# Six spectral sums handed from VectorE to accumulating DMAs, a seven-product down projection for a sixth unit, and a new order table

## The chip, the cores and the metric

The kernel runs on one core of one Trainium2 chip. The metric is the device time of one execution in microseconds, and lower is better. Before the change it is 338.21 us (median of 3 runs, 338.10 to 338.67).

## The reference

Two layers stand one behind the other, and both use the same weights. A layer is a gated long convolution (block A) and a gated feed-forward (block B), each with a layer norm in front and a residual sum behind. Tokens S = 2048, channels D = 512, feed-forward width F = 1792, everything bf16:

```python
def _A_ref(q, k, v, shift_k, ssm_k, ssm_D):
    ...                       # k_shift: causal convolution of k with 4 taps per channel
    kv = k_shift * v
    L = 2 * S
    ...                       # kv_f, kf_f: real FFTs over 2S of kv and of ssm_k, padded with zeros
    y_f = kv_f * kf_f[None, :, :, :]
    y = irfft2(y_f, ...)[:, 0, :S, :]     # causal convolution over all 2048 tokens
    y = y + kv * ssm_D[None, None, :]
    return q * y

def _B_ref(x, w_gate, w_up, w_down):
    g = _silu(x @ w_gate)
    u = x @ w_up
    return (g * u) @ w_down

x = A_q
x = x + _A_ref(_layernorm(x), A_k, A_v, A_shift_k, A_ssm_k, A_ssm_D)
x = x + _B_ref(_layernorm(x), B_w_gate, B_w_up, B_w_down)
x = x + _A_ref(_layernorm(x), A_k, A_v, A_shift_k, A_ssm_k, A_ssm_D)
x = x + _B_ref(_layernorm(x), B_w_gate, B_w_up, B_w_down)
```

The long convolution's result y depends on k, v and the filter alone, so it is computed once and used by both layers.

## The kernel before, in words

**Convolution.** The 2048 tokens are cut into NB = 4 blocks of 512. Block i of k*v gets a spectrum X[i], and two neighbouring blocks of the filter get one spectrum G[j]. Each is a tile of 128 partitions by 4096 bf16 values (1 MB): 4 slots of a real and an imaginary part of 512 channels each. The spectrum of output block k is Z[k], the sum of X[i]·G[j] over i + j = k. `product(i, j)` makes one of these terms on VectorE (DVE): two multiplications of 128x4096 (line L765, into tiles t1 and t2), and two combinations of 128x2048 (L769), a subtraction and an addition. The first product of a block writes its combinations into Z[k]. Each later one writes them back into t1, and one more DVE instruction of 128x4096 (L773) adds t1 to Z[k]. There are six of these: one for Z[1], two for Z[2], three for Z[3]. `inverse(k)` then folds Z[k] (L653, then L659 and L670, on DVE), multiplies by the inverse tables on TensorE (PE), and ScalarE (ACT) copies y out of PSUM.

**Feed-forward.** A unit (layer, c, h) is one of the two halves, 256 tokens, of block c in a layer; there are 16. `prologue` normalises, multiplies by y, adds to x, takes the statistics of the second norm, normalises to z, and has SyncE's queue (SP) transpose z into zT by DMA (L1006). `ffn` runs over four groups of 4, 4, 4 and 2 tiles of 128 of the 1792 columns: gate and up products on PE, silu and a copy on ACT (L1197, L1198, L1258, L1262), their product on DVE (L1204, L1267), and the down projection on PE. Some groups are computed with the tokens in rows, and their product hr is turned into sg by two DMA transposes from SP (L1206). The plain down projection is 28 matmuls of 512 columns for a unit (L1287), and ACT copies (L1332) and one DVE addition (L1339) bring it into x.

**Seven products.** For the units in the table STRASSEN, `seven` takes for two column tiles and two token rows seven products of 256 columns where the plain form takes eight (as 4 matmuls of 512). The operands need sums in front: on DVE three instructions a group (L1076, L1078, L1080, into cb), and once for all units sums of the down weights (L1061). The results land in four PSUM banks, and `add_seven` brings them into x with four ACT copies (L1109) and five DVE instructions (L1114 to L1121). Before the change five units work in this way: (1,2,1), (0,3,0), (0,3,1) and (1,3,0) in all four groups, (1,3,1) in two.

**Statistics.** A norm's mean and variance come either from DVE (L926, L927) or from ACT (L941, L950, L954); the tables ST1 and ST2 choose per unit. GpSimd (POOL) raises the variance to the power -1/2 (L912) for both.

**Order.** No scheduler decides at build time what runs when: every step is recorded with its engine, a cost and its buffers, and the table ORDER gives each step its place. Engines follow that order, each on its own queue, and wait for each other by semaphores. `walk` replays the steps with their costs in that order and chooses the buffer slot of each tile; in it a DMA transpose that is issued beside a load lands later (`late == 2` and `landed`).

Of the kernel before, what the change touches and what calls it, by code (L numbers as in the profile page):

```python
# [9 lines left out]
P = 128  # L10
# [11 lines left out]
ST2 = lambda l, c, h: (l, c, h) in {(0, 0, 0), (0, 2, 1), (1, 2, 1)}  # L22
K_ACT = lambda b: b in {2, 3}
PW = 0.7
# [6 lines left out]
STRASSEN={(1,2,1):4,(0,3,0):4,(0,3,1):4,(1,3,0):4,(1,3,1):2}  # L31
# [1574 lines left out]
```

## Time and profile before

| what | value |
|---|---|
| runs | 338.67, 338.10, 338.21 us; median 338.21 |
| profiled execution | span 337.1 us from the first to the last instruction; its own time is not on the page, and the median run is 1.1 us above its span |
| TensorE (PE) | busy 332.4 us (99% of the span), 2300 matmuls recorded |
| VectorE (DVE) | busy 314.3 us (93%), 566 instructions |
| ScalarE (ACT) | busy 269.4 us (80%), 550 instructions |
| GpSimd (POOL) | busy 36.1 us (11%), 48 instructions |
| DMA | 31.08 MB, mean 92 GB/s |
| granted PE clock | 1.00 |

Matmuls follow each other before the one ahead has ended: 4 matmuls of 512 columns start within 0.86 us, though each of them counts as 379 ns. So a matmul's price is read from the chain (time for a number of matmuls in a row), and a DVE instruction's price from the starts in the timeline, not from the mean length.

### The profile page before, as it was taken

The page shows a single profiled execution, that of the slowest core. Times are in us where ns is not written, and L with a number is a line of the kernel's source. Part 1 is how long each engine was busy: PE and PEld are TensorE (multiplying, and loading weights), DVE is VectorE, ACT ScalarE, POOL GpSimd, SP SyncE. Part 2 cuts the span into 40 slices and gives each one's busy share as a digit, 9 for nine tenths or more (in the row PEclk, how much of TensorE's full clock was granted, in tenths as well). Part 3 has the DMA queues.
Part 4 walks back from the last instruction along what each step waited for, and adds up shares of the span by engine and source line. Part 5 has one row for each costly group of instructions (what it writes and reads, how often), then busy time and mean ns, then how long its engine had stood idle before and what let it go on. Part 6 is the DMA issues. An engine that isn't in the chain of part 4 may idle for free.

```text
span 337.1 us, 6249 instructions
## 1 busy us (share of the span) xinstructions
PE 332.4 (99%) x2300; PEld 208.0 (62%) x2300; DVE 314.3 (93%) x566; ACT 269.4 (80%) x550; POOL 36.1 (11%) x48
## 2 busy tenths in 40 slices
PE   9999999999999999999999999999999999999996
PEld 7665865645445564644545474654445787878994
DVE  7799999999999999999999999997898998986995
ACT  6999999999966684989999794989765748476862
POOL 4010100031210100022110200021000000000000
PEclk9999999999999999999999999999999999999999
DMA  7999403632354446253314433320415320203001
GB/s 278 331 281 387 65 3 77 140 93 34 78 94 86 95 88 146 72 80 74 69 33 83 104 81 102 81 53 10 84 33 95 65 65 16 42 8 64 2 33 62
DMA packets 75817, 31.08 MB, mean 92 GB/s; under 512 B 67589, under 2 KB 73610, under 8 KB 75786
## 3 DMA queue, kind: packets, MB, share of 16 engines
q1 hardware_dynamic: 75632, 30.61, 38.3%
q8 instruction: 18, 0.29, 0.4%
q14 instruction: 13, 0.11, 0.1%
q10 hardware_dynamic: 154, 0.07, 0.1%
HBM read 12.33 MB, written 2.10 MB: 43 GB/s over the span
## 4 chain that ended last, share of the span: by engine, by line
PE 85%; DVE 10%; ACT 2%; issue 1%; POOL 0%; POOLq 0%
PE pf L423 48%; PE pd L1287 19%; PE ps L1097 7%; PE ps L423 6%; PE pf L1171 4%; DVE t L755 1%; PE wm L1572 1%; DVE Z L759 1%; DVE bst L926 1%; DVE t L769 1%; ACT jk L950 1%; DVE Z L773 1%; DVE t L765 1%; DVE m L896 1%; DVE z L976 1%
## 5 line engine op out<-in xcount | busy, mean ns | idle before, releaser
L423 PEld LDWEIGHTS <-zT 128*128 128x128 bf16 x496 | 48.5, 98 | 55.1 <-issue 0.2
L423 PE MATMUL pf<-wu_sb,zT 128*128 128x512 bf16 x248 | 61.5, 379 | 0.0
L423 PE MATMUL pf<-wg_sb,zT 128*128 128x512 bf16 x248 | 61.4, 379 | 0.0
L423 PE MATMUL pf<-zT,wg_sb 128*128 128x256 bf16 x400 | 50.7, 273 | 0.3 <-DVE zT L1037 0.3
L1197 ACT ACTIVATE sg<-pf 128x512 bf16<-128x512 f32 x62 | 37.4, 615 | 14.9 <-PE pf L423 10.7
L1287 PE MATMUL pd<-wd_sb,sg 128*128 128x512 bf16 x200 | 48.9, 379 | 0.0
L1198 ACT CAST hr<-pf 128x512 bf16<-128x512 f32 x62 | 36.3, 599 | 12.7 <-PE pf L423 10.9
L423 PEld LDWEIGHTS <-wg_sb 128*128 128x128 bf16 x400 | 38.6, 98 | 8.3 <-issue 0.7
L765 DVE TENSOR_TENSOR t<-X,G 128x4096 bf16<-128x4096 bf16 x18 | 41.0, 2287 | 0.1
L1258 ACT ACTIVATE sg<-pf 128x512 bf16<-128x512 f32 x50 | 29.6, 603 | 7.7 <-PE pf L423 6.3
L423 PE MATMUL pf<-zT,wu_sb 128*128 128x256 bf16 x272 | 34.9, 273 | 0.1
L912 POOL TENSOR_TENSOR rstd<-mv,nhalf 128x2 f32<-128x2 f32 x20 | 18.3, 919 | 147.8 <-DVE mv L927 147.8
L1287 PEld LDWEIGHTS <-sg 128*128 128x128 bf16 x200 | 19.6, 98 | 21.4
L423 PEld LDWEIGHTS <-wu_sb 128*128 128x128 bf16 x272 | 26.5, 98 | 6.6 <-issue 0.4
L1287 PE MATMUL pd<-wd_sb,ht 128*128 128x512 bf16 (+1 forms) x126 | 29.6, 369 | 0.0
L912 POOL TENSOR_TENSOR rstd<-ve,nhalf 128x2 f32<-128x2 f32 x12 | 13.8, 1150 | 119.6 <-ACT ve L954 119.6
L926 DVE BATCH_NORM_STATS2 bst<-xc 128x6 f32<-128x512 bf16 x40 | 26.3, 685 | 0.3
L1262 ACT CAST ht<-pf 128x512 bf16<-128x512 f32 x34 | 20.2, 599 | 1.6 <-PE pf L423 1.5
L1287 PEld LDWEIGHTS <-ht 128*128 128x128 bf16 x126 | 12.3, 98 | 13.4 <-DVE ht L1267 0.4
L532 ACT ACTIVATE X<-ps 128x512 bf16<-128x512 f32 x32 | 18.6, 606 | 2.3 <-PE ps L423 1.6
L1267 DVE TENSOR_TENSOR ht<-ht,sg 128x1024 bf16<-128x1024 bf16 (+1 forms) x33 | 18.3, 556 | 0.7 <-ACT sg L1258 0.4
L1204 DVE TENSOR_TENSOR hr<-hr,sg 128x1024 bf16<-128x1024 bf16 x25 | 17.1, 683 | 1.3 <-ACT sg L1197 0.9
(157 smaller groups left out, 590.9 us busy)
## 6 DMA issues: line engine op xcount, KB each, us to landing
hn<-in_A_ssm_k_dram SPq DMA_DIRECT2D x4, 512.0 KB, 4.0
vt<-in_A_v_dram SPq DMA_DIRECT2D x4, 512.0 KB, 6.0
xc<-in_A_q_dram SPq DMA_DIRECT2D x4, 512.0 KB, 5.3
out_dram<-xc SPq DMA_DIRECT2D x15, 128.0 KB, 1.9
wg_sb<-in_B_w_gate_dram SPq DMA_DIRECT2D x1, 1792.0 KB
wu_sb<-in_B_w_up_dram SPq DMA_DIRECT2D x1, 1792.0 KB, 7.6
wd_sb<-in_B_w_down_dram SPq DMA_DIRECT2D x1, 1280.0 KB, 11.5
sg<-hr SPq DMA_TRANSPOSE x62, 2.4
```

The source lines that it names most:

```text
L423: nc.tensor.matmul(o, lhsT=lhsT, rhs=rhs, start=(n == 0), stop=(n == len(terms) - 1))
L532: add("ACT", act(D), lambda: nc.scalar.activation(out=view(), in_=ps.t[:], func=ACT.Copy, scale=scale), r=[ps], w=[(buf, keys)], conv=conv)
L765: dve(8 * D, lambda t=t, part=part: nc.vector.tensor_mul(out=t.t[:], in0=x.t[:, :, part:part + 1, :].to_broadcast((P, R, 2, D)), in1=g.t[: ...
L912: add("POOL", cost, lambda: nc.gpsimd.tensor_tensor(out=rstd.t[:], in0=var(), in1=nhalf.t[:].to_broadcast((P, n)), op=ALU.pow), r=reads + ...
L926: add("DVE", 0.6, lambda st=st, i=i: nc.vector.bn_stats(out=st.t[:, 0:6], in_=xs[c].t[:, i, :]), r=[(xs[c], (i,))], w=[st])
L1097: nc.tensor.matmul(bank.t[:, half_ * C:(half_ + 1) * C], lhsT=lhsT(i), rhs=rhs(i), start=(first and i == 0 and half_ == 0), stop=(last and ...
L1197: add("ACT", act(D), lambda ps=ps, dst=dst, o=o, which=which: nc.scalar.activation(out=rows(dst, o), in_=ps.t[:], func=ACT.Silu) if which ...
L1198: out=rows(dst, o), in_=ps.t[:], func=ACT.Silu) if which == "g" else nc.scalar.copy(out=rows(dst, o), in_=ps.t[:]),
L1258: add("ACT", act(D), lambda ps=ps, o=o, sg=sg: nc.scalar.activation(out=sg.t[:, o:o + 2, :], in_=ps.t[:], func=ACT.Silu), r=[ps], w=[(sg, ...
L1262: add("ACT", act(D), lambda ps=ps, o=o, ht=ht: nc.scalar.copy(out=ht.t[:, o:o + 2, :], in_=ps.t[:]), r=[ps], w=[(ht, (o // 2,))], due=(uni ...
L1267: dve(n * W, lambda sg=sg, ht=ht: nc.vector.tensor_mul(out=ht.t[:], in0=ht.t[:], in1=sg.t[:]), [sg], [ht], due=(unit, k / pairs, 0.0, "h"))
L1287: nc.tensor.matmul((pds[o] if not cs.start else pds[HP]).t[:, cs], lhsT=ht.tiles(q, o), rhs=wt["d"].t[:, ft, cs], start=(ft == std0 and no ...
```

## The change

Four things change at once.

1. `Z_DMA` is true for every pair (i, j): the six additions L773 on DVE become six DMAs that GpSimd issues (`accum_op=ALU.add`, from t1 into Z[k], both in SBUF). `walk` gets a rule for them: a transpose that follows one is taken to land after it (`late == 5`).
2. `STRASSEN` gets (1,2,0) with all four groups: a sixth unit with seven products.
3. `ST2` loses (1,2,1): the second norm of that unit takes its statistics on DVE.
4. Scratch `jk` gets a second slot, `fq` moves into the ring of z, and ORDER is a new table of 1822 places (1798 before).

```diff
-ST2 = lambda l, c, h: (l, c, h) in {(0, 0, 0), (0, 2, 1), (1, 2, 1)}
+ST2 = lambda l, c, h: (l, c, h) in {(0, 0, 0), (0, 2, 1)}
 K_ACT = lambda b: b in {2, 3}
+Z_DMA = lambda i, j: True
...
-STRASSEN={(1,2,1):4,(0,3,0):4,(0,3,1):4,(1,3,0):4,(1,3,1):2}
+STRASSEN={(1,2,0):4,(1,2,1):4,(0,3,0):4,(0,3,1):4,(1,3,0):4,(1,3,1):2}
...
 ORDER = [
-    13, 127, 133, 202, 6, 0, 2, 4, 21, 5, 8, 1, 3, 9, 11, 17, 12, 18, 14, 19, 22, 20, 25, 24, 23, 26, 27, 37, 28, 31, 38, 69, 36, 60, 16, 52, 44,
...
+    15, 1, 0, 60, 5, 2, 13, 28, 25, 4, 6, 3, 7, 8, 9, 17, 18, 16, 14, 19, 26, 22, 21, 23, 20, 24, 37, 27, 47, 10, 11, 12, 51, 52, 56, 58,
...
+        if eng == "POOL" and lat is not None:
+            o.late = 5
...
+            if o.late == 5:
+                landed = max(landed, o.start + 9.4)
...
-    plan = Plan({"h": 1, "k": 1, "v": 1, "hs": 1, "dg": 1, "x": 2, "y": 2, "s8":11, "n": 2, "jk": 1, "dn": 1, "ks": 2, "z": 3, "zT":3,
+    plan = Plan({"h": 1, "k": 1, "v": 1, "hs": 1, "dg": 1, "x": 2, "y": 2, "s8":11, "n": 2, "jk": 2, "dn": 1, "ks": 2, "z": 3, "zT":3,
...
-    m4, fq = whole("m4", [P, R], F32), whole("fq", [P, P], F32)
+    m4, fq = whole("m4", [P, R], F32), new("z", "fq", [P, P], F32)
...
-        if not first:
+        if not first and Z_DMA(i, j):
+            add("POOL", 1.3, lambda: nc.gpsimd.dma_start(out=z.t[:], in_=t1.t[:], accum_op=ALU.add, max_dma_last_dim=4096), r=[t1], w=[z], lat=8.3, conv=conv)
+        elif not first:
             dve(8 * D, lambda: nc.vector.tensor_add(out=z.t[:], in0=z.t[:], in1=t1.t[:]), [t1], [z], conv=conv)
```

In the changed file the lines above 400 are 9 further down than before, and those above 780 are 11 further down: L653, L765, L769 are L662, L774, L778 there, and L912, L926, L1267 are L923, L937, L1278. The three places below are quoted with each file's own lines.

**VectorE where Z[1] is completed, before.** t_1096 is the second product of Z[1] (X_640 is X[1], G_255 is G[0]); Z in the first of these rows is Z[1]:

```order
L769 TENSOR_TENSOR t_1096<-t_1096,t_995 128x4x512 x2
L765 TENSOR_TENSOR t_1130<-X_640,G_703 128x4096
L773 TENSOR_TENSOR Z<-Z,t_1096 128x4096
L1339 TENSOR_TENSOR xc<-xc,dn 128x1024
L926 BN_STATS bst<-xc 128x6 x2
L927 BN_AGGR mv<-bst 128x2 x2
L653 TENSOR_TENSOR m<-Z 128x2048 x2
```

The same place of the change; t_955 is the product that is to be added, and the addition is on another engine:

```order
L778 TENSOR_TENSOR t_955<-t_955,t_1091 128x4x512 x2
L774 TENSOR_TENSOR t_1142<-X_636,G_663 128x4096
L1350 TENSOR_TENSOR xc<-xc,dn 128x1024
L937 BN_STATS bst<-xc 128x6 x2
L938 BN_AGGR mv<-bst 128x2 x3
L987 TENSOR_SCALAR n<-xc,nm,rstd 128x512 x2
L938 BN_AGGR mv<-bst 128x2
L1215 TENSOR_TENSOR hr<-hr,sg 128x1024
L987 TENSOR_SCALAR n<-xc,mv,rstd 128x512 x2
L1009 TENSOR_TENSOR n<-n,Yk 128x1024
L1010 TENSOR_TENSOR xc<-xc,n 128x1024
L937 BN_STATS bst<-xc 128x6 x2
```

Behind these rows stand two L938 and one L987, and only then the fold L662 m<-Z. So the addition has left this queue, and norm and prologue steps have moved between the product and the fold that reads the sum.

**GpSimd at the same place, before.** Every row is a power of a variance:

```order
L912 TENSOR_TENSOR rstd_989<-ve_961,nhalf_122 128x2
L912 TENSOR_TENSOR rstd_1061<-mv_1056,nhalf_122 128x2
L912 TENSOR_TENSOR rstd_1177<-ve_1147,nhalf_122 128x2
L912 TENSOR_TENSOR rstd_1191<-mv_1187,nhalf_122 128x2
L912 TENSOR_TENSOR rstd_1322<-mv_1302,nhalf_122 128x2
```

And with the change; Z_911 is Z[1], t1_955 the product above, Z_1554 is Z[2]:

```order
L923 TENSOR_TENSOR rstd_1018<-mv_1015,nhalf_95 128x2
L782 DMA Z_911<-t1_955 128x2x2048
L923 TENSOR_TENSOR rstd_1174<-ve_1137,nhalf_95 128x2
L923 TENSOR_TENSOR rstd_1197<-mv_1161,nhalf_95 128x2
L923 TENSOR_TENSOR rstd_1226<-mv_1171,nhalf_95 128x2
L923 TENSOR_TENSOR rstd_1232<-mv_1209,nhalf_95 128x2
L923 TENSOR_TENSOR rstd_1424<-mv_1399,nhalf_95 128x2
L923 TENSOR_TENSOR rstd_1604<-mv_1489,nhalf_95 128x2
L782 DMA Z_1554<-t1_1646 128x2x2048
L782 DMA Z_1554<-t1_1790 128x2x2048
L923 TENSOR_TENSOR rstd_1899<-ve_1832,nhalf_95 128x2
```

The DMAs have come into GpSimd's queue between the powers, and a power that stands behind one is issued after it.

**VectorE at the program's end, before.** The last group's product is L1267, and the rows L1114 to L1121 are the sums of the last two units:

```order
L1114 TENSOR_TENSOR xc<-xc,mt 128x1024
L1267 TENSOR_TENSOR ht<-ht,sg 128x512
L1118 TENSOR_TENSOR mt<-mt 128x512
L1119 TENSOR_TENSOR mt<-mt 128x512
L1121 TENSOR_TENSOR xc<-xc,mt 128x2x256
L1116 TENSOR_TENSOR xc<-xc,mt 128x512
L1118 TENSOR_TENSOR mt<-mt 128x512
L1119 TENSOR_TENSOR mt<-mt 128x512
L1121 TENSOR_TENSOR xc<-xc,mt 128x2x256
L1294 TENSOR_TENSOR xc<-xc,pd 128x512
L1303 TENSOR_TENSOR xc<-xc,pd 128x256
```

And with the change:

```order
L1125 TENSOR_TENSOR xc<-xc,mt 128x1024
L1129 TENSOR_TENSOR mt<-mt 128x512
L1127 TENSOR_TENSOR xc<-xc,mt 128x512
L1130 TENSOR_TENSOR mt<-mt 128x512
L1132 TENSOR_TENSOR xc<-xc,mt 128x2x256
L1278 TENSOR_TENSOR ht<-ht,sg 128x512
L1130 TENSOR_TENSOR mt<-mt 128x512
L1132 TENSOR_TENSOR xc<-xc,mt 128x2x256
L1305 TENSOR_TENSOR xc<-xc,pd 128x512
L1314 TENSOR_TENSOR xc<-xc,pd 128x256
```

The last product has moved behind one unit's sums, three instructions from the two closing additions. On PE its gate matmuls have moved as well: 8 of them now stand right ahead of the last 7 matmuls of L1108 and the 18 closing ones of L1298, where before 43 of L1097 stood in between.

142 rows, old and new, of the table ORDER are left out of this document.

## The prediction

> **What bounds the kernel now.** I read the page's first part, then the windows, then who waits, then the chain.
>
> ```profile
> PE 332.4 (99%) x2300; PEld 208.0 (62%) x2300; DVE 314.3 (93%) x566; ACT 269.4 (80%) x550; POOL 36.1 (11%) x48
> 70.00:80.00 10.00, 10.00 (x48) 4.58 (x47) 9.96 (x12) 9.96 (x21) 4.37 (x2) 1.00 0.26 71
> 250.00:260.00 10.00, 10.00 (x60) 5.59 (x59) 8.50 (x19) 6.57 (x14) 0.69 (x1) 1.00 0.36 66
> 33.00:334.00 301.00, 300.70 (x2005) 186.28 (x2005) 285.32 (x493) 240.01 (x492) 30.10 (x30) 1.00 0.32 67
> PE wm L1572 <- PEq L1590: 0.8, 1, 0.8
> PE ptz L1034 <- DVE z L976: 0.3, 1, 0.3
> PE pf L423 <- DVE zT L1037: 0.3, 1, 0.3
> ```
>
> In the windows the columns behind the length are the busy time of PE, of its weight loads, of DVE, ACT and POOL, then the granted clock. From 33 to 334 us PE is busy for 300.70 of 301.00 us at clock 1.00. The last three rows are all the waits that the waits view lists for matmuls: 1.4 us, of which 0.8 is the program's start and 0.6 lies before 33 us. Since busy ends are modelled, I check the rate in the chain (start, length, what):
>
> ```profile
> 48.50 4.32 PE pd L1287 x20
> 274.07 5.35 PE ps L1097 x49
> 311.68 1.91 PE pf L423 x16
> 315.58 1.75 PE pf L423 x16
> ```
>
> 20 matmuls of 512 columns take 4.32 us, 0.216 us each, and 49 of 256 columns 5.35 us, 0.109 each: no gaps inside. The 16 at 311.68 took 0.16 us more than the 16 at 315.58; that is as large as a hiccup gets here. So the time is PE's work in a row, and an edit counts in two ways only: by the PE work that it adds or takes away, and by any wait that it puts into this row. DVE, full in the early windows (9.96 of 10) and not in the later (8.50), is the engine that would make PE wait.
>
> **Part one: the seven products.** The unit's plain down projection is 28 matmuls of 512 columns, 28 x 0.216 = 6.05 us. With seven products it is 7 pairs of column tiles x 7 = 49 of 256 columns, and the chain's second row is just such a run: 5.35 us. That is 0.70 us less on PE, and PE is the path, so all of it counts if nothing else gives. On DVE and ACT it costs work off that path:
>
> ```profile
> L1339 DVE TENSOR_TENSOR xc<-xc,dn 128x1024 bf16<-128x1024 bf16 x11 | 7.5, 684 | 0.0
> L1114 DVE TENSOR_TENSOR xc<-xc,mt 128x1024 bf16<-128x1024 bf16 x5 | 3.4, 688 | 1.3 <-ACT mt L1109 1.3
> L1121 DVE TENSOR_TENSOR xc<-xc,mt 128x512 bf16<-128x512 bf16 x5 | 2.1, 423 | 0.1
> L1076 DVE TENSOR_TENSOR cb<-sg 128x512 bf16<-128x512 bf16 x6 | 2.5, 414 | 0.2 <-issue 0.2
> L1080 DVE TENSOR_TENSOR cb<-sg 128x256 bf16<-128x256 bf16 x6 | 1.7, 285 | 0.0
> L926 DVE BATCH_NORM_STATS2 bst<-xc 128x6 f32<-128x512 bf16 x40 | 26.3, 685 | 0.3
> L927 DVE BATCH_NORM_AGGREGATE mv<-bst 128x2 f32<-128x9 f32 x40 | 6.3, 182 | 0.2
> L773 DVE TENSOR_TENSOR Z<-Z,t 128x4096 bf16<-128x4096 bf16 x6 | 13.7, 2287 | 0.0
> ```
>
> A group of four tiles takes two instructions like L1076 and one like L1080, 1.1 us, and three groups 3.3; the last group is half as large, about 0.8. Bringing the banks in takes one like L1114 and four like L1121, 2.4 us, and the one L1339 goes: together 4.1 + 2.4 - 0.7 = 5.8 us. The norm that ST2 moves to DVE adds two L926 and two L927, 1.7 us, and frees ACT of about as many steps. So 7.5 us are added on DVE.
>
> **Part two: the six additions.** They go from DVE, 13.7 us by the last row; with the 7.5 added, DVE ends 6.2 us lighter. In itself this is worth nothing: PE doesn't wait for DVE behind 33 us. It only pays for part one. What it costs hangs on when the sum lands. I take the place where Z[1] is completed, where DVE is fullest:
>
> ```profile
> 67.81 2.35 DVE L769 TENSOR_TENSOR t<-t,t 128x2048 bf16<-128x2048 bf16 x2
> 70.08 2.29 DVE L765 TENSOR_TENSOR t<-X,G 128x4096 bf16<-128x4096 bf16 x1
> 72.28 2.29 DVE L773 TENSOR_TENSOR Z<-Z,t 128x4096 bf16<-128x4096 bf16 x1
> 74.48 0.69 DVE L1339 TENSOR_TENSOR xc<-xc,dn 128x1024 bf16<-128x1024 bf16 x1
> 75.20 1.29 DVE L926 BATCH_NORM_STATS2 bst<-xc 128x6 f32<-128x512 bf16 x2
> 76.40 0.31 DVE L927 BATCH_NORM_AGGREGATE mv<-bst 128x2 f32<-128x9 f32 x2
> 76.63 2.32 DVE L653 TENSOR_TENSOR m<-Z 128x2048 bf16<-128x2048 bf16 x2
> 80.09 0.73 DVE L976 TENSOR_SCALAR n<-xc,mv,rstd 128x512 bf16<-128x512 bf16 x2
> 82.54 0.69 DVE L999 TENSOR_TENSOR xc<-xc,n 128x1024 bf16<-128x1024 bf16 x1
> 83.14 0.42 DVE L1201 TENSOR_TENSOR hr<-hr,sg 128x512 bf16<-128x512 bf16 x1
> ```
>
> From start to start the 4096-wide multiplication takes 2.20 us, a 1024-wide step 0.60 (82.54 to 83.14), a pair of statistics 1.20, a pair of normalisations 0.65. In the change, by the order quoted above, DVE has between the finished product and the fold: one multiplication (2.20), the residual sum (0.65), two pairs of statistics (2.4), six aggregations in rows of 3, 1 and 2 (0.6), five normalisations (1.6), and three 1024-wide steps (1.9): 9.3 us. The same count gives 9.7 us ahead of Z[2]'s fold and 12.1 ahead of Z[3]'s. Whatever lands inside this cover costs nothing.
>
> The trace of before has no accumulating DMA. The nearest rows (KB each, median us from issue to landing):
>
> ```profile
> wu_sb<-in_B_w_up_dram SPq DMA_DIRECT2D x1, 1792.0 KB, 7.6
> sg<-hr SPq DMA_TRANSPOSE x62, 2.4
> kTb<-in_A_k_dram SPq DMA_TRANSPOSE x3, 8.5
> ```
>
> At the first row's rate (236 KB a us) the 1024 KB of t1 alone take 4.3 us: the lower end. If t1, the old Z and the new Z each pass in turn, 3072 KB take 13.0: the upper end. I take the two that are read as setting the pace, 2048 KB, 8.7 us: inside all three covers, by 0.6 us at the tightest, so no wait. From before's side the change loses nothing on DVE up to a landing of 9.3 + 2.2 = 11.5 us, since the addition itself stood there.
>
> The Trainium skill's page "DMA: Bandwidth & Descriptors", section "Anatomy of one DMA — SWDGE (gpsimd) path", fits 2.0 us plus the bytes at 436 GB/s; an estimate by it for 1 MB is 4.4 us, near my lower end, and the sum would be the same. No run here shows such a DMA.
>
> Issuing on GpSimd: its queue takes a DMA between two powers. A power waits at most for that issue:
>
> ```profile
> 46.51 0.69 POOL L912 TENSOR_TENSOR rstd<-mv,nhalf 128x2 f32<-128x2 f32 x1 [8.22 <-DVE mv L927]
> 72.85 2.86 POOL L912 TENSOR_TENSOR rstd<-ve,nhalf 128x2 f32<-128x2 f32 x1 [7.29 <-ACT ve L954]
> 61.65 0.58 SPq L495 DMA_DIRECT2D vt<-in_A_v_dram  x1
> ```
>
> SP needs 0.58 us for an issue; a power needs 0.69 us, and 2.86 where DVE's L773 ran beside it. I put the issue between 0.6 and 2.9 us, and take 1: GpSimd is idle for most of the span (11% busy), and the next power in the order is for a normalisation that stands behind 4.3 us of DVE work. Nothing on the path.
>
> **The ends.** Up to the first gate product the two orders have the same matmuls on PE and the same work on DVE; I count nothing, at most 0.2 us either way. At the end, the last gate product has moved towards the last down products: between them stand 7 matmuls of 256 columns and 4 of 512, 7 x 0.109 + 4 x 0.216 = 1.6 us.
>
> ```profile
> 325.50 1.04 PE L423 MATMUL pf<-zT,wg_sb 128*128 128x256 bf16 x8
> 326.58 0.60 ACT L1258 ACTIVATE sg<-pf 128x512 bf16<-128x512 f32 x1 [1.27 <-PE pf L423]
> 328.63 0.42 DVE L1267 TENSOR_TENSOR ht<-ht,sg 128x512 bf16<-128x512 bf16 x1
> ```
>
> The silu follows 0.2 us behind PE's next start (326.38) and takes 0.60, the product 0.42, with a hand-over some 1.4: hidden by 0.2 us, and at most 0.3 late if sums of the unit stand in its way on DVE.
>
> **The sum.** Profiled span 337.1, median of the runs 338.2, so 1.1 us lie around the span; I leave these as they are. 337.1 - 0.70 = 336.4 us of span, 337.5 us of time.
>
> **Rivals.**
>
> *The sum lands late (slower).* One accumulating DMA lands L us after its issue, and DVE stands at the fold of Z from 9.3 us on, with the z of the next unit's prologue and its transposes queued behind it; PE has been fed by that chain without slack, as DVE's 9.96 of 10 us in 70:80 says. The time is 337.5 + (L - 9.3) if one place passes its wait on: 339.7 at 11.5 us, 341.2 at 13.0. It decides from 9.3 us, and is slower than before by the bound from about 10.7. For: the upper end of the price, and the loads on the queues; 0.6 us of cover is little. Against: the lower end is 5 us below the cover, and later places have more.
>
> *Transposes caught beside it (slower).* A transpose of 128 KB lands in 2.4 us; the kTb transposes, issued among loads, need 8.5 for 512 KB. An hr that becomes sg while 1 MB is being added would land up to 6 us later, and the down projection that reads it stands in PE's row. If one in six DMAs catches a needed one by 2 to 3 us: 339.5 to 340.5. Against: in the order the additions mostly stand away from such pairs. The Trainium skill speaks for this rival: the page "DMA: Bandwidth & Descriptors", section "Issuing engines are not separate DMA queues", says that DMAs of all issuers run on the same 16 engines and interleave. The rows of kTb agree that a transpose gets longer among loads; how much beside an addition no trace here shows.
>
> *DVE holds the issue (slower or the same).* The power at 72.85 was held for 2.2 us by the addition on DVE. Right behind each finished product DVE starts its next 2.20 us step; if GpSimd's writing of descriptors is held like that, the DMA lands 2.2 us later, at 10.9, and DVE waits 1.6: up to 339.1. The Trainium skill's page "SBUF — State Buffer", section "SBUF: two separate sides", says that a DVE instruction in a two-port mode starves descriptors that GpSimd writes; its section "Who interferes with whom" takes two-input additions and multiplications out of this, as they hold only the reading side. By that rule the time stays 337.5. The row at 72.85 agrees for an instruction that reads; for writing descriptors no trace here decides.
>
> *More is gained.* If the 0.6 us of waits before 33 us go as well, and the hiccups with them: 336.8. Little speaks for it, since the start has the same work in another order.
>
> **How the numbers follow.** About 0.2% (0.68 us) is what a measurement of this kernel can tell from no change; so the bounds are 337.5 and 338.9, and the forecast lies on the first. Forecast 0.45, its own range 337.0 to 338.2, of which I give 0.27 to faster and 0.18 to the same. More gained 0.15, faster. Late landing 0.20, slower. Caught transposes 0.12, slower. Held issue 0.08, of which 0.05 the same and 0.03 slower. Faster 0.42, same 0.23, slower 0.35. The range leaves out the extreme gain and landings beyond 12.6 us: 336.8 to 340.8.
>
> **What would show it.** Right: L773 gone, DVE's busy time down by about 6 us, six DMAs that land within 9 us, DVE's wait for them at L662 under 0.5 us in all, PE's row from 33 us on still closed. Wrong: L662 waiting for the DMA by 2 us or more; L1298 waiting for sg<-hr; powers of over 3 us behind a DMA; PE waits of more than 1 us in all behind 33 us.

## The result, and the profile after

The changed kernel takes 343.67 us (median of 4 runs, 342.53 to 345.55) against 338.44 for the kernel before on the same chip: 1.016 times as long, 95% interval 1.012 to 1.020. The forecast was 337.5 us, its range ended at 340.8, and the change is slower.

The page's first part, the accumulating DMAs' queue, and the window of the prediction (columns as before: length, PE, its weight loads, DVE, ACT, POOL, granted clock):

```profile
PE 332.0 (97%) x2290; PEld 210.3 (61%) x2321; DVE 309.8 (90%) x580; ACT 269.2 (78%) x542; POOL 40.9 (12%) x54
q0 software_dynamic: 1632, 6.29, 10.3%
33.00:334.00 301.00, 294.15 (x1948) 183.22 (x1972) 275.75 (x497) 236.86 (x477) 35.08 (x36) 0.99 0.44 87
```

PE, which was busy for 300.70 of these 301 us, now is for 294.15. Who PE waits for, and whom the accumulating DMAs make wait on DVE:

```profile
PE pd L1298 <- DMA sg<-hr: 3.2, 1, 3.2
PE ps L432 <- DMA hs<-hr: 1.0, 1, 1.0
PE pf L432 <- DMA zT<-z: 0.7, 1, 0.7
...
DVE t L774 <- DMA Z<-t: 0.4, 1, 0.4
```

No fold L662 waits for a sum. What PE waits for are transposes, and above all one pair at 206 us. SyncE's row there, GpSimd's row, and the DMAs of 194 to 212 us with their median time to landing:

```profile
195.28 2.55 SPq L1358 DMA_DIRECT2D out_dram<-xc  x4
197.94 2.98 SPq L1017 DMA_TRANSPOSE zT<-z  x1
204.84 0.34 SPq L508 DMA_DIRECT2D xc<-in_A_q_dram  x1
205.28 2.87 SPq L1217 DMA_TRANSPOSE sg<-hr  x2
...
193.73 1.49 POOL L923 TENSOR_TENSOR rstd<-ve,nhalf 128x2 f32<-128x2 f32 x1 [26.82 <-ACT ve L965]
195.16 1.22 POOL L782 DMA_DIRECT2D Z<-t  x1
...
Z<-t POOLq DMA_DIRECT2D x1, 1024.0 KB, 8.6
out_dram<-xc SPq DMA_DIRECT2D x4, 128.0 KB, 7.5
zT<-z SPq DMA_TRANSPOSE x2, 5.7
```

The fourth accumulating DMA is issued at 195.16 us, and 0.12 us behind it the first of four outputs. The first still lands after 1.9 us, as such an output does alone (below); the third and fourth take 7.5 and 7.7, and the fourth lands at 204.69. The load of x writes the buffer that the outputs read, so SyncE holds it until 204.84, and the two transposes behind it, whose hr was ready at 201.7, go out from 205.28. PE has nothing else from 206.3 to 209.6.

What follows that wait, on PE from 210.47 us on and in the window of the 14 matmuls behind the wait:

```profile
210.47 2.57 PE L1298 MATMUL pd<-wd_sb,ht 128*128 128x512 bf16 x6
212.83 1.65 PE L1298 MATMUL pd<-wd_sb,sg 128*128 128x512 bf16 x4
214.31 1.46 PE L1298 MATMUL pd<-wd_sb,ht 128*128 128x512 bf16 x6
...
209.59:214.31 4.72, 4.72 (x14) 1.82 (x15) 4.58 (x5) 2.96 (x9) 0.21 (x1) 0.64 0.12 23
```

The granted clock is 0.64 in the mean of this window. From start to start the ten matmuls from 210.47 on take 3.84 us instead of 10 x 0.216 = 2.16: another 1.7 us. Two of the four runs have a mean clock of 0.995 (344.7 and 345.55 us) and two of 0.999 and 1.0 (342.5 and 342.65), so this loss comes and goes.

**The 6.7 us of the profiled span** (343.8 against 337.1): counted from start to start of the matmuls behind 33 us, PE stands still for 6.35 us instead of 0.40. That is 3.41 at 206 us, 1.16 at 63, 0.82 at 154, 0.48 at 114 and small ones. With 1.7 us for the clock this is 7.65; the rest is about -1 us. Of this 0.70 is what the seven products take less by their count of matmuls; where the last 0.3 us lie is not shown.

### The profile page after: what moved, and what is told of

Same layout as the page of the kernel before. It is cut to its first block, busy times and chain, and to the rows that moved or that the text cites. A ratio compares the mean times of both kernels' runs of the same rounds, so it can differ in the third digit from the quotient of the medians.

```text
span 343.8 us, 6273 instructions
## 1 busy us (share of the span) xinstructions
PE 332.0 (97%) x2290; PEld 210.3 (61%) x2321; DVE 309.8 (90%) x580; ACT 269.2 (78%) x542; POOL 40.9 (12%) x54
## 4 chain that ended last, share of the span: by engine, by line
PE 75%; ACT 12%; DMA 5%; DVE 4%; issue 2%; SPq 2%; ACTq 0%; DVEq 0%
PE pf L432 40%; PE pd L1298 14%; PE ps L1108 8%; PE ps L432 5%; PE pf L1182 3%; DMA sg<-hr 2%; PE ps L580 2%; ACT n L982 2%; ACT X L541 1%; DMA hs<-hr 1%; DVE t L774 1%; DMA zT<-z 1%; ACT ht L1273 1%; ACT H L541 1%; PE wm L1583 1%
## 5 line engine op out<-in xcount | busy, mean ns | idle before, releaser
L432 PE MATMUL pf<-zT,wg_sb 128*128 128x256 bf16 x400 | 49.9, 273 | 0.1
L1298 PE MATMUL pd<-wd_sb,sg 128*128 128x512 bf16 x169 | 42.2, 383 | 3.6 <-DMA sg<-hr 3.2
L774 DVE TENSOR_TENSOR t<-X,G 128x4096 bf16<-128x4096 bf16 x18 | 41.0, 2284 | 0.5 <-DMA Z<-t 0.4
L923 POOL TENSOR_TENSOR rstd<-mv,nhalf 128x2 f32<-128x2 f32 x21 | 19.4, 923 | 145.4 <-DVE mv L938 140.3
L432 PE MATMUL pf<-zT,wu_sb 128*128 128x256 bf16 x272 | 34.1, 273 | 0.1
L1298 PEld LDWEIGHTS <-sg 128*128 128x128 bf16 x176 | 17.3, 99 | 23.3 <-DMA sg<-hr 3.7
L937 DVE BATCH_NORM_STATS2 bst<-xc 128x6 f32<-128x512 bf16 x42 | 27.5, 683 | 2.9 <-DMA xc<-in_A_q_dram 2.5
L1298 PE MATMUL pd<-wd_sb,ht 128*128 128x512 bf16 (+1 forms) x121 | 28.8, 380 | 0.1
L923 POOL TENSOR_TENSOR rstd<-ve,nhalf 128x2 f32<-128x2 f32 x11 | 11.1, 1011 | 89.7 <-ACT ve L965 89.7
L1108 PEld LDWEIGHTS <-cb 128*128 128x128 bf16 x195 | 18.6, 98 | 3.3 <-DVE cb L1091 0.4
L541 ACT ACTIVATE X<-ps 128x512 bf16<-128x512 f32 x32 | 19.4, 619 | 1.3 <-PE ps L580 0.5
L1298 PEld LDWEIGHTS <-ht 128*128 128x128 bf16 x122 | 12.2, 100 | 13.4 <-issue 1.1
```

The lines of the kernel that those rows point to most:

```text
L432: nc.tensor.matmul(o, lhsT=lhsT, rhs=rhs, start=(n == 0), stop=(n == len(terms) - 1))
L541: add("ACT", act(D), lambda: nc.scalar.activation(out=view(), in_=ps.t[:], func=ACT.Copy, scale=scale), r=[ps], w=[(buf, keys)], conv=conv)
L774: dve(8 * D, lambda t=t, part=part: nc.vector.tensor_mul(out=t.t[:], in0=x.t[:, :, part:part + 1, :].to_broadcast((P, R, 2, D)), in1=g.t[: ...
L923: add("POOL", cost, lambda: nc.gpsimd.tensor_tensor(out=rstd.t[:], in0=var(), in1=nhalf.t[:].to_broadcast((P, n)), op=ALU.pow), r=reads + ...
L937: add("DVE", 0.6, lambda st=st, i=i: nc.vector.bn_stats(out=st.t[:, 0:6], in_=xs[c].t[:, i, :]), r=[(xs[c], (i,))], w=[st])
L1108: nc.tensor.matmul(bank.t[:, half_ * C:(half_ + 1) * C], lhsT=lhsT(i), rhs=rhs(i), start=(first and i == 0 and half_ == 0), stop=(last and ...
```

## The experiments

Theory A: the fourth accumulating DMA delays what is issued beside it, and that makes the loss at 206 us. Theory B: the new order alone does it. Theory C, tested by the first experiment: taking VectorE's 13.7 us off was worth something. `moved(ORDER, (a, b))` below puts step a right behind step b and leaves all else.

**All six additions on VectorE again, in the new order.**

```diff
-Z_DMA = lambda i, j: True
+Z_DMA = lambda i, j: False
```

> All six additions go back to VectorE, in the places where the changed order has the accumulating DMAs; everything else is the changed kernel. Theory A (the accumulating DMA issued at 195 us holds back the four output DMAs issued just behind it, these hold SyncE at the load of x, and the transposes behind it leave TensorE idle for 3.2 us at 206 us, after which its clock is halved for 3.4 us): that wait falls under 0.5 us and the clock stays at 1.0; the waits of 1.2 us at 63 us and 0.8 us at 154 us stay, since no accumulating DMA is near them; time 338.0 to 339.5. Theory B (the new order alone makes the loss): the wait at 206 us stays at 3 us or so and the time at 342 or more. Theory C (VectorE's 6 x 2.29 = 13.7 us were worth taking off): the folds behind the additions come late, TensorE waits 1 us or more for them at two places or more, time above 341.

350.55 us, 1.036 (1.034 to 1.038). The wait at 206 us is down to 0.3 us (at 211), but behind 33 us PE now stands still for over 0.25 us at eleven places, 12.7 us in all. The page's first row and PE's longest wait:

```profile
PE 333.1 (95%) x2321; PEld 208.5 (60%) x2321; DVE 322.4 (92%) x586; ACT 268.6 (77%) x542; POOL 41.3 (12%) x48
PE pf L432 <- ACT sg L1208: 2.3, 1, 2.3
```

Theory C came nearest, though none of these waits is at a fold. At the places which the new table gives them, the additions cost 6.9 us more on VectorE than as DMAs. That the table is laid out for a VectorE without these 13.7 us is the likely reading; an order with the additions at other places was not tried.

**Only the fourth sum on VectorE.**

```diff
-Z_DMA = lambda i, j: True
+Z_DMA = lambda i, j: (i, j) != (2, 1)
```

> Only the fourth accumulating DMA, the one of 195 us, becomes an addition on VectorE (2.29 us); the other five stay DMAs. Theory A: the same as with all six on VectorE, 338.0 to 339.5, no wait of more than 0.5 us at 206 us, clock 1.0. If each of the six DMAs costs a share of the loss, only a part comes back: 341 to 342.5. Theory B: 342 or more.

341.87 us, 1.011 (1.009 to 1.012), clock 1.0. The DMAs from 194 to 212 us, and PE's waits:

```profile
out_dram<-xc SPq DMA_DIRECT2D x4, 128.0 KB, 1.9
xc<-in_A_q_dram SPq DMA_DIRECT2D x1, 512.0 KB, 4.0
...
PE ps L432 <- DMA hs<-hr: 1.2, 1, 1.2
PE ps L432 <- DVE vt L738: 1.1, 1, 1.1
PE pd L1298 <- DMA sg<-hr: 0.7, 1, 0.7
```

Without the DMA the outputs land in 1.9 us and the load of x goes out at 200.4. The wait at 206 us falls from 3.2 to 0.7 and the clock stays up, so theory B is out for this place. The addition now stands in VectorE's row, ahead of a vt that PE waits 1.1 us for. That took back part of the gain: theory A expected 338.0 to 339.5, measured 341.9. The time alone would also fit the other expectation, in which each of the six DMAs costs a share (341 to 342.5); PE's waits speak against it, as none of over 0.25 us falls into the flight of one of the other five here.

**The transposes ahead of the load, all DMAs kept.**

```diff
-        plan.issue(*plan.order(ORDER), 6.0, warm)
+        plan.issue(*plan.order(moved(ORDER, (1109, 1116), (1110, 1109))), 6.0, warm)
```

> All six accumulating DMAs stay. In SyncE's row the load of x of 204.8 us and the two transposes behind it change places. Theory A, with the held queue as the link: the two transposes are issued at 201.7 us, when their data are ready, instead of 205.3, land before 206.5, TensorE's wait there falls under 1 us, clock 1.0; the outputs still take over 6 us to land beside the accumulating DMA; time 338.5 to 340. Rival (the transposes' own packets are caught beside the accumulating DMA, which the trace has busy until 203.3): they take 5 us or more to land, TensorE waits 1.5 us or more, time above 340.5.

343.76 us, 1.016 (1.014 to 1.018), clock 1.0 in all runs. The transposes go out at 200.5 and 202.9 us and land after 5.6 and 3.7. DMAs from 194 to 206 us, PE's and DVE's waits (lines are 11 further down in kernels with `moved`):

```profile
out_dram<-xc SPq DMA_DIRECT2D x4, 128.0 KB, 7.5
sg<-hr SPq DMA_TRANSPOSE x3, 4.6
...
PE pd L1309 <- DVE ht L1289: 2.0, 1, 2.0
PE pd L1309 <- DMA sg<-hr: 1.7, 2, 1.4
...
DVE bst L948 <- DMA xc<-in_A_q_dram: 4.7, 1, 4.7
```

One wait of 3.2 became two: for transposes that land late, and for a VectorE that now waits 4.7 us for x. The rival's 1.5 us was reached; holding SyncE's row is not the whole of it.

**All six as DMAs in the kernel before.** Its order and products stay.

```diff
-        if not first:
+        if not first and Z_DMA(i, j):
+            add("POOL", 1.3, lambda: nc.gpsimd.dma_start(out=z.t[:], in_=t1.t[:], accum_op=ALU.add, ...), r=[t1], w=[z], lat=8.3, conv=conv)
+        elif not first:
```

> The kernel before, its order unchanged and without the sixth unit's seven products, with the six additions as accumulating DMAs where VectorE had them. The folds stand 4.3, 2.3 and 2.3 us behind the additions' start there, so with 8.1 us to landing and some 1.3 us of issue VectorE must wait about 5, 7 and 7 us for Z, against 13.7 us that it no longer adds. Theory A: above 339, most of it from these waits, and any output or load issued beside a DMA lands late. Theory B (accumulating DMAs harmless, the new order at fault): 337.5 to 338.5.

369.18 us, 1.091 (1.088 to 1.095). The folds wait, as expected, if longer: 23.7 us in all, against some 19. On PE transposes come on top (the last row is what DVE waits for):

```profile
PE pd L1290 <- DMA sg<-hr: 10.0, 3, 4.8
...
DVE m L654 <- DMA Z<-t: 23.7, 3, 10.8
```

**The fourth DMA one inverse root later.** `moved(ORDER, (651, 1306))`

> All six accumulating DMAs stay; only the fourth is put one place later in GpSimd's row, behind the next inverse root, so that it is issued some 13 us later, when the four outputs, the load of x and the transposes of 195 to 208 us are through and SyncE has nothing to issue until 222 us. Its buffer is free for that long and the next sum waits for it. Theory A (what the fourth DMA meets, not the DMAs as such): outputs of 195 us land in 2 us, the load of x is issued by 201, TensorE's wait at 206 us falls under 0.5 us, clock 1.0; the waits at 63 and 154 us stay; 339.0 to 340.3. If the DMA only carries its trouble with it (the fifth sum then lands late, near 226 us, beside the transposes of 222 us): a wait of 1 us or more at 222 to 232 us and over 341.

346.98 us, 1.026 (1.024 to 1.027). At 206 us everything happened as theory A says: outputs land in 2.1 us or less, the load goes out at 199.0, no wait. But now the fourth DMA runs from 210.9 to 219.1 us, the fifth adds to the same Z and stands in GpSimd's row waiting for it, with an inverse root behind it, and then runs beside the later of the transposes of 217 us, which wait for that root. That is the second expectation, trouble carried along. GpSimd's row, and PE's wait at 224 us:

```profile
210.88 1.22 POOL L793 DMA_DIRECT2D Z<-t  x1
219.96 1.20 POOL L793 DMA_DIRECT2D Z<-t  x1 [7.86 <-ACT sg L1280]
220.71 1.19 POOL L934 TENSOR_TENSOR rstd<-ve,nhalf 128x2 f32<-128x2 f32 x1
...
PE pd L1309 <- DMA sg<-hr: 4.4, 1, 4.4
```

**Two rows moved where no accumulating DMA runs.** `moved(ORDER, (543, 540), (813, 815))`

> The changed kernel with two rows moved where no accumulating DMA runs: the last hs<-hr transpose goes ahead of the loads of hn and v that stand before it in SyncE's row at 58 us, and the second z of 150 us goes ahead of one ka and two n in ScalarE's row. If the waits at 63 us (1.2) and 154 us (0.8) are the new order's own: both fall under 0.3, the wait at 206 us stays near 3 us, and the time falls by 1.5 to 2, to 341.3 to 342.5. If the time that TensorE waits there is only passed on (the loads come late, the DMAs meet other work): less than 0.7 us is gained.

345.02 us, 1.019 (1.015 to 1.023): no gain in time. All four runs have a lowered clock (0.99 or 0.995; in the trace it falls behind the wait at 206 us, which stays at 3.3 us), so the median says little about 1.5 us: the two at 0.995 took 343.06 and 344.20, against 344.7 and 345.55 for the changed kernel's two at that clock. The trace says more: from start to start the wait at 154 us is gone (0.82 before), that at 63 us is passed on to the sg<-hr transposes behind (1.16, now 0.77).

**Packets a quarter as long.** `max_dma_last_dim=4096` becomes `1024`.

> The accumulating DMAs move the same bytes between the same places in packets a quarter as long. If other transfers wait behind whole packets of 4 KB, the four outputs beside the fourth DMA land in under 4 us instead of 7.5, the load of x is issued 3 us earlier, the wait at 206 us falls to 1 us or less, and the time to 340 to 341.5, even if the DMA itself takes longer. If they share by time or by descriptor (four times as many of them), the outputs land as late or later, and the time is 343.5 or more.

348.65 us, 1.032 (1.027 to 1.037). Queue, and DMAs from 194 to 215 us:

```profile
q0 software_dynamic: 6240, 6.29, 12.3%
...
Z<-t POOLq DMA_DIRECT2D x1, 1024.0 KB, 10.7
out_dram<-xc SPq DMA_DIRECT2D x4, 128.0 KB, 4.0
```

The outputs land in 4.0 us in the median instead of 7.5, as expected if others wait behind whole packets, and not if they share by time or by descriptor. The time is where that rival had it all the same: the DMAs got longer (one 13.5 us, for which a multiplication on VectorE waits 4.4), transposes still take 4.2 us (sg<-hr) and 5.9 (zT<-z) in that stretch, and PE stands still for 3.6 us at two places. The Trainium skill, page "DMA: Bandwidth & Descriptors", section "Queues, rings and completion order", says that each DMA engine takes turns between its queues at packet boundaries; 7.5 against 4.0 us agrees.

**Later DMA and both moved rows.** `moved(ORDER, (651, 1306), (543, 540), (813, 815))`

> The later fourth DMA and the two moved rows together. If the three places are independent and are the whole of the loss: no wait of TensorE above 0.5 us behind 33 us, 337.2 to 338.6, near the kernel before less the 0.70 us of the seven products. If more is at fault than these three: above 339.5.

346.13 us, 1.024 (1.021 to 1.027). The long wait, 4.56 us, is at 222 us now; the three places are not independent of where the DMA goes.

**x in a buffer of its own.**

```diff
-        xs[c] = new("x", "xc", [P, R, D], parts=R + 2)
+        xs[c] = new("y" if c == 3 else "x", "xc", [P, R, D], parts=R + 2)
```

> The changed kernel, order untouched, but the fourth chunk of x is loaded into a buffer that nobody else needs then, so that the load no longer waits for the four outputs. The outputs still land 7.5 us after their issue beside the fourth accumulating DMA. Theory A (the loss at 206 us runs through SyncE held at that load): the load is issued by 201 us and the two transposes at 201.7; what then remains is what the moved load left, some 1.6 us from transposes that land late beside the DMA, without the 2.2 us that VectorE waited for the late x; wait at 206 us 0.5 to 1.7, clock 1.0, time 340 to 341.5. Rival (the packets of load and transposes are themselves caught, the queue only shows it): wait above 2.5 us and over 342.5.

344.14 us, 1.018 (1.016 to 1.019). The load goes out at 200.34 and the transposes from 201.92, as theory A wanted, and PE waits as long as before. The DMAs issued from 200 to 210 us, and PE's wait:

```profile
xc<-in_A_q_dram SPq DMA_DIRECT2D x1, 512.0 KB, 7.6
sg<-hr SPq DMA_TRANSPOSE x2, 6.5
...
PE pd L1298 <- DMA sg<-hr: 3.2, 1, 3.2
```

So the held queue was one path among several. Load and transposes are caught themselves: the rival holds. The accumulating DMA is not the only one to catch them: it lands at 203.2, and the second transpose, issued at 204.0, still takes 4.9 us beside the late load.

**The same, and both moved rows.** `moved(ORDER, (543, 540), (813, 815))` as well

> The same buffer for x, and the two moved rows of 58 and 150 us. If the three places are the loss: 338.3 to 340.3, no single wait of TensorE above 1.7 us, clock 1.0. If the moved rows only pass the time on, as long waits with a lowered clock hid in the last run with them: within 0.4 us of the run without them.

343.10 us, 1.014 (1.013 to 1.016). PE's wait at 206 us is 3.3 us still; behind 33 us its waits of over 0.25 us are 5.0 us instead of 5.9, and the time is 1.0 us less than without the moved rows, a part of it by the clock (two of the four runs at 1.0, none without them). The wait at 154 us is gone again, so it is the new order's own; that at 63 us is passed on again (1.1 us).

**The fifth DMA behind the root.** `moved(ORDER, (651, 1306), (1015, 1185))`

> The fourth accumulating DMA one inverse root later, as before, and now the fifth one behind the next inverse root too. Theory (GpSimd works its row in order: the fifth DMA, waiting for the fourth to land, held the inverse root behind it, and n, hr and the transposes waited for that): the root is no longer late, TensorE's wait of 4.6 us at 224 us falls under 1.5, clock 1.0, time 340 to 342. Rival (the transposes of 217 to 228 us are late because the fifth DMA runs beside them): it runs beside them still, the wait stays above 2.5 us and the time above 343.

345.88 us, 1.022 (1.021 to 1.024). The root is no longer late, at 215.45 instead of 220.71 us, and PE's wait stays. GpSimd's row, DMAs from 215 to 230 us, PE's wait:

```profile
215.45 0.71 POOL L934 TENSOR_TENSOR rstd<-ve,nhalf 128x2 f32<-128x2 f32 x1 [4.29 <-ACT sg L1219]
218.54 1.22 POOL L793 DMA_DIRECT2D Z<-t  x1 [2.38 <-DMA Z<-t]
...
sg<-hr SPq DMA_TRANSPOSE x4, 8.3
...
PE pd L1309 <- DMA sg<-hr: 4.5, 1, 4.5
```

The rival is right again: the transposes run beside the two DMAs and take 8.3 us in the median. The theory was not wrong about the kernel with the later DMA, where PE's wait does run through the late root; but with the root early the third transpose goes out at 219.10 instead of 224.08, right behind the fifth DMA, and needs until 228.2. Either alone is enough for the wait.

**One DMA in the kernel before.** As with all six, but

```diff
+Z_DMA = lambda i, j: (i, j) == (2, 1)
```

> The kernel before, order and products untouched; of its six additions only the fourth becomes an accumulating DMA. Nothing needs its sum for 15 us, so no landing is waited for, and VectorE does 2.29 us less. Contention theory: zT<-z and sg<-hr issued while it runs (some 188 to 198 us) land in 4 us or more instead of 2.4, TensorE waits 1 to 4 us there, 339.5 to 343. If the new order is needed for the loss: transposes land as before and the time is 337.8 to 338.4.

340.36 us, 1.006 (1.004 to 1.008). The first two rows are DMAs of 188 to 198 us in this kernel, the third the same in the kernel before, and the last is PE's wait in this one:

```profile
Z<-t POOLq DMA_DIRECT2D x1, 1024.0 KB, 8.7
zT<-z SPq DMA_TRANSPOSE x2, 6.6
```

```profile
zT<-z SPq DMA_TRANSPOSE x2, 2.4
```

```profile
PE pf L424 <- DMA zT<-z: 1.6, 1, 1.6
```

Nothing else was changed and nobody waits for the sum: one accumulating DMA makes the two zT<-z land after 6.6 us in the median instead of 2.4 and costs 2.1 us. The new order is not needed for a loss of this kind.

**Five DMAs, the fourth sum on VectorE at a later place.** With `(2, 1)` on VectorE: `moved(ORDER, (651, 1133), (543, 540), (813, 815), (616, 383), (290, 616))`

> The changed kernel with the fourth sum added on VectorE, behind the next xc addition instead of in the DMA's place; the hs<-hr transpose ahead of its neighbours and the second z ahead in ScalarE's row; and the loads of hn and v of 58 us behind the four sg<-hr transposes of 61 us. If the named places are all of the loss: TensorE's waits behind 33 us sum to under 1.5 us and the time is 337.8 to 338.9. If the five other DMAs cost time of their own: above 339.5.

345.51 us, 1.020 (1.017 to 1.024). The late sum puts the fifth DMA at 215.97 us, and the transposes of 220.69 us beside it: 2.7 us on PE. The loads, now at 66 us, and the first DMA at 70 us run beside the zT<-z of 67 us: 2.1 us. So new collisions hide the answer that was asked for.

**The same, at an earlier place, loads unmoved.** `moved(ORDER, (651, 1128), (543, 540), (813, 815))`

> The same, but the loads of hn and v stay, and the fourth sum is added 10 us or so earlier, behind the second product of SwiGLU's last group. Some 0.8 to 1.1 us of waiting at 64 us stays, so 338.5 to 339.8 if the named places are the whole loss; above 340 if not.

340.84 us, 1.008 (1.006 to 1.010), the best of the new order. GpSimd's row, SyncE's row, and PE's longest wait behind 33 us:

```profile
209.90 1.22 POOL L793 DMA_DIRECT2D Z<-t  x1
...
218.69 5.69 SPq L1228 DMA_TRANSPOSE sg<-hr  x4
...
PE pd L1309 <- DMA sg<-hr: 1.0, 1, 1.0
```

Here the fifth DMA, 209.90 to some 218 us, fits into the stretch in which SyncE issues nothing, and no transpose there is late. PE still stands still for 3.2 us behind 33 us, at 65 us (1.2), 114 (0.5) and 205 to 216 (1.4), and these account for the time: the span is 1.5 us above the profiled one of before, 2.8 us more of waiting less about 1 us of matmuls. By its own expectation (above 340) the named places are not the whole loss: small waits for ScalarE at 114, 215 and 216 us, 1.6 us together, were not in it. No version of these is faster than the kernel before.

## Why the prediction was wrong

- **PE's row sets the time: right.** The spans worked out above come out of PE's waits, its clock and its matmuls, to some 0.3 us.
- **Seven products, -0.70 us: right, as far as the traces tell.** Such a run of 49 still takes 5.35 us in the chain. PE's row behind 33 us less its waits is 300.2 us before and 299.8 with one DMA in the old order; it is 298.7 to 299.7 in the four profiled kernels of the new order whose clock stayed at 1.0. A part of that spread is the cut at 33 us. Three of the four have a record of every matmul: against the kernel before, 7 more of 256 columns lie ahead of the cut (3 with all sums on VectorE), 0.76 us (0.33). With these set aside the term is 0.3 to 0.8 us.
- **VectorE ends 6.2 us lighter: right.** The lines in question sum to 6.3 us less. The page's busy time, in which overlaps count once, fell by 4.5.
- **Landing price 8.7 us, no fold waits: right.** The six took 7.9 to 9.5 us, median 8.1, and DVE waited 0.4 us in all, none of it at a fold. That two of three passes set the pace is not shown, since no run changes the bytes alone; in so far the price was a lucky choice between 4.3 and 13.0. In the kernel before, where the covers are 2 to 4 us, the folds waited 23.7: the covers counted in the order were needed.
- **"In itself this is worth nothing": wrong in the new order.** With the additions back on VectorE it is 6.9 us slower. The sentence was read off the kernel before, where PE waits for nothing behind 33 us; it was not true of the changed one.
- **The step that failed: the sum has no term for what an addition in flight delays, because "in the order the additions mostly stand away from such pairs".** Of five of the six that was true: in their flights PE never stands still for more than 0.25 us. The fourth made the sentence worthless, because it reads one queue's order as if it were time. That DMA's data were ready at 177.4 us; it stood in GpSimd's row behind an inverse root released at 193.7, and so started at 195.16, just ahead of four outputs, a load and three transposes in SyncE's row.
- **The rival "transposes caught beside it" had the cause, and half of the path.** In the changed kernel the outputs are caught, they hold the load, and the load holds the transposes in SyncE's row. The transposes are caught themselves once they go out earlier (medians 4.6 and 6.5 us in two experiments). The rule of the Trainium skill quoted for this rival holds (2.4 us against medians of 4.2 to 8.3 beside a DMA, in six kernels). It was priced at 2 to 3 us and given 0.12; it was 3.4 us, and 1.7 more in the profiled run by the clock. The engine to watch was wrong too: the prediction named DVE, and of PE's waits behind 33 us all but 0.6 us are for transposes.
- **Two terms were missing.** The clock behind a long wait, 1.7 us. And the new order's own waits at 63, 114 and 154 us, 2.5 us together: I compared VectorE's and GpSimd's rows and the program's ends, not SyncE's and ScalarE's. No accumulating DMA is in flight at any of the three (up to there they fly from 70.5 to 78.6 us, from 122.7 to 132.2 and from 137.2 to 145.4), and the first two waits stay with all sums on VectorE (1.4 and 1.1 us). At 63 us a transpose PE needs stands behind two loads of 512 KB; at 154 us a z stands in ScalarE's row behind one step of the convolution and two normalisations.
- **Held issue: fell.** The six issues took 1.2 to 1.4 us, and VectorE waits for a root 0.9 us at most, the same with the DMAs and with all sums on VectorE.

## What to carry to other kernels

An operation handed to a DMA leaves its engine, but for its whole flight (8 us for 1 MB here) it delays what the DMA engines carry beside it: price it by what is issued in those microseconds on every queue, at the time that its own queue's order gives it, not when its data are ready. Place it in a stretch in which no transfer feeds the row that sets the time: 210 to 218 us held such a DMA for nothing here, and 195 to 204 us cost 3.4, and 5.1 where the clock fell. An engine that is freed is worth something only to an order that uses it, and that order brings waits of its own on the other queues.

## What the runs showed of the hardware

- 1 MB added from SBUF to SBUF by an accumulating DMA lands 7.8 to 10.7 us after its issue in 4 KB packets, and takes GpSimd 1.2 to 1.4 us to issue; with packets a quarter as long 8.2 to 13.5 and 1.5 to 1.7. The prediction's estimate from the Trainium skill's page "DMA: Bandwidth & Descriptors", 4.4 us, is half of it.
- Beside one, an output of 128 KB takes 7.5 us in the median instead of 1.9, a load of 512 KB 7.6 instead of 4.0, a transpose 4.6 to 8.3 in the median instead of 2.4. What is caught delays others in turn, so these are prices of a place, not of the DMA alone.
- Behind a wait, PE's clock is halved in the traces for whole multiples of 3.41 us. It came behind the wait of 3.4 us in the profiled run of the changed kernel, while two of its other runs show no lowered clock; of the sixteen runs of the four kernels whose trace has a wait of 3.4 to 3.5 us at this place, twelve show one. The three kernels with a wait of 4.6 to 4.7 us have it in all twelve runs, in the traces for 3.41 or 6.83 us. Shorter ones are not safe: waits of 2.2 to 2.5 us from start to start passed unpunished in three kernels, while in the kernel with the sum at the later place one of 2.3 us (2.1 us idle) did not (PE's row, then the window with the clock):

```profile
72.74 1.36 PE L443 MATMUL pf<-wg_sb,zT 128*128 128x512 bf16 x4 [2.11 <-DMA zT<-z]
...
72.50:76.50 4.00, 3.76 (x11) 1.42 (x12) 2.23 (x8) 1.32 (x3) 1.38 (x2) 0.60 1.03 179
```

The Trainium skill, page "TensorE: Matmul & The Clock Gate", section "What's actually happening", gives half clock after an idle window of about 3.4 us, with windows that run freely. The multiples of 3.41 us and the chance in it agree. That a whole window must be idle does not: the clock falls at 73.3 us, and in the 3.41 us ahead of that PE was idle for 2.1.
